# Token statistics of four more tiles on ScalarE, a weight expansion on GpSimd, the last product in two halves, and a new instruction order

## The chip, the cores and the metric

The kernel runs on one core of one Trainium2 chip. The metric is the device time of one execution in microseconds. One execution was also recorded by the hardware profiler; its rows are what the text argues from. The engines are called by what they do in the profile: PE is TensorE's matmuls and PEld its weight loads, DVE is VectorE, ACT is ScalarE, POOL is GpSimd, SP is SyncE, whose queue issues nearly all DMAs.

## The reference

Two layers over a sequence of S = 2048 tokens of width D = 640, in bf16. The first is a linear attention of H = 32 heads of width 20, with softmax feature maps; the second a bilinear gated feed-forward of width F = 1536. Both have a layer norm ahead and a residual around them.

```python
def _layernorm(x, axis=-1, eps=1e-5):
    m = jnp.mean(x, axis=axis, keepdims=True)
    v = jnp.var(x, axis=axis, keepdims=True)
    return (x - m) / jnp.sqrt(v + eps)

def _A_ref(x, wqkv, w_phi, wo):
    q, k, v = ...                      # x @ wqkv, split into 32 heads of 20
    pq = jnp.einsum("bhsd,hdf->bhsf", q, w_phi)
    pk = jnp.einsum("bhsd,hdf->bhsf", k, w_phi)
    phi_q = jnp.concatenate([_softmax(pq, axis=-1), _softmax(-pq, axis=-1)], axis=-1)
    phi_k = jnp.concatenate([_softmax(pk, axis=-1), _softmax(-pk, axis=-1)], axis=-1)
    kv = jnp.einsum("bhsf,bhsd->bhfd", phi_k, v)
    z  = jnp.einsum("bhsf->bhf", phi_k)
    num = jnp.einsum("bhqf,bhfd->bhqd", phi_q, kv)
    den = jnp.einsum("bhqf,bhf->bhq", phi_q, z)[..., None] + 1e-6
    return (num / den, heads side by side) @ wo

def _B_ref(x, w_gate, w_up, w_down):
    g = jnp.einsum("bsd,df->bsf", x, w_gate)
    u = jnp.einsum("bsd,df->bsf", x, w_up)
    return jnp.einsum("bsf,fd->bsd", g * u, w_down)

h  = x + _A_ref(_layernorm(x, axis=-1), A_wqkv, A_w_phi, A_wo)
h2 = h + _B_ref(_layernorm(h, axis=-1), B_w_gate, B_w_up, B_w_down)
```

## The kernel before, in words

The tokens are cut into 16 tiles of 128. Everything stays in SBUF from the loads to the last store. The kernel is written as a list of operations (`g.op`), each with its engine, what it reads and writes, the buffers it uses, and a planner's estimate of its length (`t`), of the time until others may use its result (`lat`), and, for DMAs, of the size. Nothing of that order reaches the chip as it is written: the table `ORDER` holds for each engine a string of unit names, and the n-th mention of a unit takes the n-th operation of that unit on that engine. So each engine's queue is written out by hand (or by a program), the engines run their queues strictly in order, and semaphores between them are placed where one needs another. The estimates decide only which of a pool's buffers an operation gets. Transposes and loads have eight semaphores each in turn (rings `tr` and `w`), stores of the result four (`out`). After its last DMA, SP waits for the last user of each of the twenty.

The units that the text speaks of:

- `wk`, `x0` to `x4`: the key weights are multiplied with the feature map's weights before any token is seen. `wk` are transposed chunks of the key weights with their column means, `x0` to `x4` the products. They need the expanded feature weights `Phi`, five pieces `a` (line 636), each a small product of two SBUF tensors; pieces 0 to 2 are made on VectorE, 3 and 4 on GpSimd. `y0` to `y4` do the same for the query weights, after five transposed loads `t0` to `t4` and mean additions `wq0` to `wq4`.
- `s0`, `s2`, `s4`, `s8`, `s12` (function `stats`): mean and square sum of the tokens, for 2, 2, 4, 4 and 4 tiles. There are two ways. For most, TensorE multiplies the transposed tile with itself and a column of ones, in five matmuls of 129 columns, and VectorE takes the diagonal of the product (line 702, one reduction a tile). For batches named in `ST_ACT`, TensorE only makes the column of sums, in five matmuls of one column, and ScalarE squares the untransposed tile with a running sum (line 650). The rest is small work on GpSimd.
- `k`, `v`, `q` with a tile number: products for keys, values and queries; VectorE takes a maximum for the exponentials and scales it (lines 925, 928), ScalarE takes two exponentials a tile for keys and queries (line 933) and copies the values. `K` and `Q`: sums of the features (lines 947, 987) and the scaling of the features, on GpSimd (line 950 for keys). `A`: the product of keys and values, in parts of two tiles, which ends this first part; `Aout` copies it.
- `n`, `h`: attention output of a tile, and its product with Wo, residual and second layer norm. `wo0` to `wo4`: row sums of Wo on ScalarE (line 650 too).
- `f`: the feed-forward's gate and up products. `d`, `D`: the down product; `D3.1` is the last, for tiles 14 and 15. A `D` unit makes seven half-size products into PSUM that are combined by additions on VectorE (lines 1332, 1342), with intermediate copies on ScalarE and additions on GpSimd.
- `lT4` to `lT15`: transposed loads of token tiles. `lx0` to `lx3`: plain loads of four token tiles each into `x_all` (640 KB). `lwq`, `lwo`, `lg`, `lu`, `ld`: weights.

PSUM is four buffers of two banks (`p_ps`), reused as soon as the engine that reads a product is done. The part of the last unit that the change rewrites is, before:

```python
mm(v2, 1, raw(3), wsum_(3), True)
fin(v2, 1, o2_, 0, c_)
store(o2_, t2)
mm(v2, 0, summed(3), wraw(3), False)
fin(v2, 0, o1_, 1, b_)
store(o1_, t1, 2 if b == NB - 1 else 1)
```

Of the kernel before, what the change touches and what calls it, by code (L numbers as in the profile page):

```python
# [1499 lines left out]
```

## Time and profile before

| what | value |
|---|---|
| runs, median (lowest to highest) | 267.58 us (267.44 to 268.17) |
| profiled execution | 267.55 us |
| its span, first to last instruction | 265.8 us |
| granted TensorE clock | 0.999 |
| TensorE busy | 260.4 us, 98% |
| VectorE, GpSimd, ScalarE busy | 222.7, 190.1, 177.2 us |
| DMA | 28.65 MB, mean 108 GB/s |

How to read it: the busy time of TensorE includes waits that matmuls hide in their pipeline, so the share alone does not say that it is at its limit. A row of the timeline gives start, length, engine, line, operation, result and sources with their sizes, and the number of instructions merged; a bracket at its end gives the idle time of that engine just before it and what ended it. A row of a window gives its length, then busy time and instruction count for PE, PEld, DVE, ACT and POOL, the clock, the share of the DMA engines and GB/s.

### The profile page before, as it was taken

The page shows a single profiled execution, that of the slowest core. Times are in us where ns is not written, and L with a number is a line of the kernel's source. Part 1 is how long each engine was busy: PE and PEld are TensorE (multiplying, and loading weights), DVE is VectorE, ACT ScalarE, POOL GpSimd, SP SyncE. Part 2 cuts the span into 40 slices and gives each one's busy share as a digit, 9 for nine tenths or more (in the row PEclk, how much of TensorE's full clock was granted, in tenths as well). Part 3 has the DMA queues.
Part 4 walks back from the last instruction along what each step waited for, and adds up shares of the span by engine and source line. Part 5 has one row for each costly group of instructions (what it writes and reads, how often), then busy time and mean ns, then how long its engine had stood idle before and what let it go on. Part 6 is the DMA issues. An engine that isn't in the chain of part 4 may idle for free.

```text
span 265.8 us, 6243 instructions
## 1 busy us (share of the span) xinstructions
PE 260.4 (98%) x2418; PEld 200.0 (75%) x2433; DVE 222.7 (84%) x417; ACT 177.2 (67%) x387; POOL 190.1 (72%) x243
## 2 busy tenths in 40 slices
PE   8999999999999999999999999999999999999995
PEld 8877777776877787777767887777777777777773
DVE  1999999999999876998999778988778788675683
ACT  2567999999857998769553695764857555645220
POOL 5446989999932889999974789359866575648652
PEclk9999999999999999999999999999999999999999
DMA  7997999903155789666856515300410401001012
GB/s 188 302 138 175 165 233 401 382 32 75 39 82 100 89 247 210 130 106 133 131 115 128 47 25 79 99 4 0 56 45 19 83 0 52 1 2 51 14 65 71
DMA packets 67390, 28.65 MB, mean 108 GB/s; under 512 B 57632, under 2 KB 66080, under 8 KB 67360
## 3 DMA queue, kind: packets, MB, share of 16 engines
q1 hardware_dynamic: 66432, 27.90, 48.7%
q10 hardware_dynamic: 928, 0.35, 0.5%
q8 instruction: 19, 0.31, 0.5%
q14 instruction: 11, 0.09, 0.1%
HBM read 11.82 MB, written 2.62 MB: 54 GB/s over the span
## 4 chain that ended last, share of the span: by engine, by line
PE 85%; DVE 5%; DMA 3%; ACT 3%; issue 1%; POOL 1%; SPq 0%; ACTq 0%
PE ps L657 60%; PE ps L1210 24%; DMA phiqT<-eq 3%; ACT eq L933 1%; DVE ob L1075 1%; PE ps L746 1%; DVE x_all L1093 1%; DVE ps L925 1%; DVE Sq L987 1%; ACT phiqT L1335 0%; POOL eq L999 0%; DVE rden L1073 0%; DVE phiqT L806 0%; ACT junk L650 0%; ACT eq L1220 0%
## 5 line engine op out<-in xcount | busy, mean ns | idle before, releaser
L657 PE MATMUL ps<-Wp,xT 128*128 128x320 bf16 (+1 forms) x606 | 89.1, 299 | 0.0
L657 PEld LDWEIGHTS ps<-Wp,xT 128*128 128x128 bf16 x606 | 58.0, 98 | 22.5 <-ACT phik L933 0.3
L1240 POOL TENSOR_TENSOR phik<-phik,gate 128x512 bf16<-128x512 bf16 x34 | 40.1, 1184 | 25.9 <-DVE phik L1237 25.5
L1220 ACT ACTIVATE eq<-ps 128x256 f32<-128x256 f32 x110 | 37.4, 386 | 23.0 <-PE ps L1210 18.6
L1210 PE MATMUL ps<-phik,Wgu 128*128 128x256 bf16 (+1 forms) x214 | 46.6, 299 | 0.2
L950 POOL TENSOR_TENSOR phik<-phik,Rk 128x1280 bf16<-128x1280 bf16 x16 | 37.4, 2357 | 5.8 <-DVE Rk L949 4.8
L657 PE MATMUL ps<-phik,Wgu 128*128 128x256 bf16 (+1 forms) x259 | 33.2, 280 | 0.1
L657 PEld LDWEIGHTS ps<-phik,Wgu 128*128 128x128 bf16 x260 | 25.0, 98 | 5.5
L1337 POOL TENSOR_TENSOR phiqT<-phiqT,x_all 128x320 f32<-128x320 f32 x26 | 21.7, 844 | 9.7 <-ACT phiqT L1335 9.6
L925 DVE TENSOR_REDUCE ps<-ps 128x1 f32<-128x640 f32 (+1 forms) x32 | 26.1, 818 | 2.8 <-PE ps L657 2.8
L1210 PEld LDWEIGHTS ps<-phik,Wgu 128*128 128x128 bf16 x228 | 21.9, 98 | 5.7 <-ACT eq L1220 0.2
L657 PE MATMUL ps<-vaug,phik 128*128 128x63 bf16 (+1 forms) x308 | 25.9, 238 | 0.0
L987 DVE TENSOR_REDUCE Sq<-eq 128x66 f32<-128x1320 bf16 x16 | 24.2, 1513 | 1.4 <-ACT eq L933 1.4
L1237 DVE TENSOR_TENSOR phik<-ps,eq 128x512 bf16<-128x512 f32 x28 | 19.1, 687 | 6.3 <-PE ps L1210 6.2
L1335 ACT ACTIVATE phiqT<-ps 128x320 f32<-128x320 f32 x26 | 11.4, 437 | 19.3 <-PE ps L657 19.2
L947 DVE TENSOR_REDUCE Ssum<-phik 128x64 f32<-128x1280 bf16 x16 | 23.3, 1460 | 0.0
L1235 DVE TENSOR_TENSOR gate<-ps,eq 128x512 bf16<-128x512 f32 x27 | 18.5, 685 | 5.2 <-PE ps L1210 2.9
L657 PEld LDWEIGHTS ps<-vaug,phik 128*128 128x128 bf16 x308 | 18.1, 97 | 5.3
L999 POOL TENSOR_TENSOR eq<-eq,rq 128x660 bf16<-128x660 bf16 x16 | 20.9, 1305 | 0.8
L933 ACT ACTIVATE eq<-ps,nb,rs 128x300 bf16<-128x300 f32 (+2 forms) x26 | 17.2, 689 | 6.1 <-DVE nb L928 4.5
L1342 DVE TENSOR_TENSOR outb<-ps,phiqT 128x320 bf16<-128x320 f32 x28 | 13.4, 487 | 6.9 <-PE ps L657 5.5
L1139 ACT ACTIVATE gate<-ps 128x256 bf16<-128x256 f32 (+1 forms) x26 | 10.4, 406 | 10.3 <-PE ps L657 9.6
(168 smaller groups left out, 526.2 us busy)
## 6 DMA issues: line engine op xcount, KB each, us to landing
x_all<-in_A_x_dram SPq DMA_DIRECT2D x4, 640.0 KB, 10.7
out_dram<-outb SPq DMA_DIRECT2D x14, 160.0 KB, 1.9
Wgu<-in_B_w_gate_dram SPq DMA_DIRECT2D x1, 1920.0 KB, 10.6
Wgu<-in_B_w_up_dram SPq DMA_DIRECT2D x1, 1920.0 KB, 16.3
vaug<-in_B_w_down_dram SPq DMA_DIRECT2D x1, 1920.0 KB, 8.5
Wp<-in_A_wqkv_dram SPq DMA_DIRECT2D x1, 800.0 KB, 5.0
phiqT<-in_A_wqkv_dram SPq DMA_DIRECT2D x1, 800.0 KB, 6.4
Wo<-in_A_wo_dram SPq DMA_DIRECT2D x1, 800.0 KB, 6.0
```

The costliest lines, as they stand in the source:

```text
L657: ins = e.matmul(o_, lhsT=l_, rhs=r_, start=s_, stop=p_, skip_group_check=True)
L925: g.op("DVE", lambda e: e.tensor_reduce(out=mx(), in_=src(), axis=AX.XY if len(src().shape) == 3 else AX.X, op=ALU.max, apply_absolute_val ...
L933: g.op("ACT", lambda e, s=s, sc=sc, to=to, of=of: e.activation(out=to(s), in_=of(), func=ACT.Exp, bias=nb[:, i:i + 1], scale=sc[:, t:t + 1 ...
L947: g.op("DVE", lambda e: e.tensor_reduce(out=Ssum[:, vs.i, :], in_=x, axis=AX.X, op=ALU.add), rd=R_phik[t], wr=vs.R, use=[vs], t=1.39, lat=1.5)
L950: g.op("POOL", lambda e: e.tensor_tensor(out=x, in0=x, in1=Rk[:, vr.i, :].unsqueeze(2).to_broadcast([P, 2 * H, DH]), op=ALU.mult), rd=vr.R ...
L987: g.op("DVE", lambda e: e.tensor_reduce(out=Sq[:, vs.i, :].rearrange("p (w g) -> p w g", w=NQ), in_=feat(0, NQ).rearrange("p w (g f) -> p ...
L999: return e.tensor_tensor(out=x, in0=x, in1=rq[:, vr.i, :].rearrange("p (w h) -> p w h", h=HW).unsqueeze(3).to_broadcast([P, NQ, HW, DH]), ...
L1210: ins = e.matmul(o_, lhsT=l_[0](c), rhs=m_, start=fr, stop=False, skip_group_check=True)
L1220: g.op("ACT", lambda e: e.activation(out=half(s[i], 256 * h, 256 * (h + 1)), in_=PS[v.i][:, bk, 256:512], func=ACT.Copy), rd=[v.R[bk]], wr ...
L1237: g.op("DVE", lambda e: e.tensor_tensor(out=hhT[:, hb_, ft, :], in0=PS[v.i][:, 1, :], in1=half(s[1]), op=ALU.add), rd=[v.R[1]] + s[1].R, w ...
L1240: g.op(eng, lambda e: e.tensor_tensor(out=hhT[:, hb_, ft, :], in0=hhT[:, hb_, ft, :], in1=gate[:, vg.i, :], op=ALU.mult), rd=R_out + vg.R, ...
L1337: g.op("POOL", lambda e: e.tensor_tensor(out=slot(x), in0=slot(x), in1=x_all[:, t, c], op=ALU.add), rd=x.R + [R_h[t]], wr=x.R, use=[x], t= ...
```

## The change

`ST_ACT` names batch 8 besides 12, so tiles 8 to 11 take the second way. The third piece of `Phi` moves from VectorE to GpSimd. In the last `D` unit the product that is made last is another one, and it is cut into two halves of 160 columns, each added and stored by itself; the stores of that unit go out in pieces, some of them on ScalarE's queue. All five engines' orders are new. The planner's estimates for loads and transposes are changed, which only matters for how buffers are dealt out.

```diff
-ST_ACT = (12,)
+ST_ACT = (8, 12)
...
-        g.op("DVE" if a < 3 else "POOL", phi_op, t=0.42, rd=[R_Wrows, R_G[a]], wr=[R_Phi[a]])
+        g.op("DVE" if a < 2 else "POOL", phi_op, t=0.42, rd=[R_Wrows, R_G[a]], wr=[R_Phi[a]])
...
-        def store(o_, t, parts=1):
+        def store(o_, t, parts=1, by=("SP", "SP")):
...
-                g.op("SP", lambda e, k=k: e.dma_start(out[0, P * t:P * (t + 1), n * k:n * (k + 1)], outb[:, o_.i, n * k:n * (k + 1)]),
+                g.op(by[k], lambda e, k=k: e.dma_start(out[0, P * t:P * (t + 1), n * k:n * (k + 1)], outb[:, o_.i, n * k:n * (k + 1)]),
...
+        if (b, i) == (NB - 1, 1):
+            g.op("SP", lambda e: e.dma_start(out[0, P * t2:P * (t2 + 1), HALF:D], outb[:, o2_.i, HALF:D]), rd=[o2_.R[1]], use=[o2_],
+                 dma=("w", 8), t=0.45, lat=0.1, size=0.2)
+        if (b, i) == (NB - 1, 1):
+            mm(v2, 0, summed(3), wraw(3), False)
+            fin(v2, 0, o1_, 1, b_)
+            store(o1_, t1, 2, ("SP", "ACT"))
+            l_, r_, q = raw(3), wsum_(3), HALF // 2
+            o_ = o2_
+            for k, (vk, bk) in enumerate(((v2, 1), (v1, 1))):
+                g.op("PE", lambda e, k=k, vk=vk, bk=bk: mms(e, [(PS[vk.i][:, bk, 0:q], l_[0](ft), r_[0](ft)[:, q * k:q * (k + 1)], ft == 0, False)
+                                                                for ft in range(KH)]), rd=l_[1] + r_[1], wr=[vk.R[bk]], use=[vk], t=0.415, lat=0.565)
+                R_q = Reg()
+                g.op("DVE", ...)       # adds PS[vk][:, bk, 0:q] and its part of c_ into outb
+                g.op(("ACT", "SP")[k], ...)       # stores these 160 columns
+            return
```

The orders, cut to the stretches that the prediction speaks of (TensorE's opening and the part about the statistics of tiles 8 to 11, ScalarE's middle, SP's loads, VectorE around `q7`):

```diff
 PE
-"warm wk wk wk wk wk wk wk wk wk s0 wk x1 s0 x1 x3 wv wv x2 x0 x0 s2 x4 s2 k0 ... s4 s4 s4 s4 v5 k7 v7 k4 k6 v4 k5 y3 v0 y1 s8 s8 s8 s8 y4 k10 y2 y0 v1 s12 ..."
+"warm wk wk wk wk wk wk wk wk wk x0 wk x1 x0 x1 s0 x3 s0 wv wv x2 x4 s2 s2 k0 ... s4 s4 s4 s4 k7 v4 v5 v7 k4 y1 k6 k5 y3 v0 s8 s8 s8 s8 k10 y4 y2 v1 s12 ..."
-"... f0.6.0 q10 f0.2.0 f0.3.0 q9 f0.9.0 f0.3.0 f0.9.0 n4 ..."
+"... q10 n5 f0.3.0 f0.3.0 f0.6.0 f0.6.0 n4 q9 f0.9.0 ..."
 ACT
-"... k1 v2 v3 k3 k2 wq1 k2 v5 wq3 k7 v7 k7 k4 k4 v4 k6 k6 k5 v0 k5 s12 ..."
+"... k1 v3 v2 k1 k2 s8 k2 s8 wq1 wq3 v5 v4 v7 k7 k7 k4 k4 s8 k6 s8 k5 v0 k6 k5 y4 y2 s12 ..."
-"... wo0 v14 k12 k12 v10 k13 wo1 k13 v13 k14 k14 wo2 v8 k15 k15 v15 q2 wo4 ..."
+"... wo2 v12 wo3 v10 k14 k14 k15 k15 q2 q2 v15 wo2 v8 q3 q3 wo0 wo1 wo4 ..."
 DVE
-"... n1 n1 q7 Q5 q7 Q5 q4 ..."
+"... n1 n1 q7 n1 q7 Q5 q4 ..."
 SP
-"in in in in in in in lwq t4 lT7 lT4 t2 lT5 lT6 t3 t1 t0 lx3 lT10 lT15 lT9 lT11 lT8 lT13 lT14 lT12 lx0 lwo lg lu lx2 lx1 Q0 ..."
+"in in in in in in in lT4 lwq lT6 lT5 lT7 lx2 t2 t3 t1 lT11 t0 t4 lx3 lT9 lT8 lT10 lT13 lT15 lT12 lT14 lx0 lwo lu lg Q1 Q0 Q1 Q0 lx1 ..."
```

More of the change, by code (lines that the diff above doesn't have):

```diff
@@ L587, in load_xT @@
     def load_xT(t, at=0.0):
-        transpose(lambda: xT[:, t, :, 0:P], lambda: A_x[0, P * t:P * (t + 1), :], [], [R_xT[t]], t=1.5, size=0.75, lat=1.25 if at else 2.75, at=at)
+        transpose(lambda: xT[:, t, :, 0:P], lambda: A_x[0, P * t:P * (t + 1), :], [], [R_xT[t]], t=1.5 if at else 1.4, size=0.75 if at else 0.62, lat=1.25 if at else 2.1, at=at)
     def load_x(b):
-        load(x_all[:, 4 * b:4 * b + 4, :], A_x[0, 4 * P * b:4 * P * (b + 1), :].rearrange("(t p) n -> p t n", p=P), [R_x[b]], 1.2)
+        load(x_all[:, 4 * b:4 * b + 4, :], A_x[0, 4 * P * b:4 * P * (b + 1), :].rearrange("(t p) n -> p t n", p=P), [R_x[b]], 0.9)
     def load_wv(c0, c1, at):
@@ L686, in f @@
                 return mms(e, lst)
-            g.op("PE", f, rd=[R_xT[t], R_one, R_xone], wr=[v.R[j // 2]], use=[v], t=0.125 if act else 0.282, lat=0.275 if act else 0.43)
+            g.op("PE", f, rd=[R_xT[t], R_one, R_xone], wr=[v.R[j // 2]], use=[v], t=0.19 if act else 0.282, lat=0.34 if act else 0.43)
             if act:
@@ L818, in wq_means @@
         v = Buf(p_ps, 2)
[L819 removed]
+        g.op("PE", lambda e: mms(e, mean_mms(PS[v.i][:, 0, :], range(NC), 0)), rd=R_Wnat + [R_one], wr=v.R, use=[v], t=0.73, lat=0.88)
         g.op("ACT", lambda e: e.activation(out=nmeanq[:, :], in_=PS[v.i][:, 0, 0:NC], func=ACT.Copy, scale=-1.0 / SC),
@@ L1362, in down_pair @@
         fin(v1, 0, o2_, 1, d_, [c_])
+        if (b, i) == (NB - 1, 1):
[11 more added lines that the diff above has]
+                R_q = Reg()
+                g.op("DVE", lambda e, k=k, vk=vk, bk=bk: e.tensor_tensor(
+                    out=outb[:, o_.i, q * k:q * (k + 1)], in0=PS[vk.i][:, bk, 0:q], in1=slot(c_)[:, q * k:q * (k + 1)], op=ALU.add),
+                    rd=[vk.R[bk]] + c_.R, wr=[R_q], use=[vk, o_, c_], t=0.28, lat=0.4)
+                g.op(("ACT", "SP")[k], lambda e, k=k: e.dma_start(out[0, P * t2:P * (t2 + 1), q * k:q * (k + 1)], outb[:, o_.i, q * k:q * (k + 1)]),
+                     rd=[R_q], use=[o_], dma=("w", 8), t=0.45, lat=0.1, size=0.1)
+            return
         mm(v2, 1, raw(3), wsum_(3), True)
@@ L1385, in _build @@
     U("lwo")
-    load(Wo[:, :, 0:D], A_wo.rearrange("(c p) n -> p c n", p=P), R_Wo, 1.5)
+    load(Wo[:, :, 0:D], A_wo.rearrange("(c p) n -> p c n", p=P), R_Wo, 0.95)
     for b in range(NB):
```

9 lines of the change are left out of this document (4 added, 5 removed), and 134 rows, old and new, of the table ORDER.

## The prediction

> **What bounds the kernel now.** I read the page first: busy time per engine, then the chain that ended last.
>
> ```profile
> PE 260.4 (98%) x2418; PEld 200.0 (75%) x2433; DVE 222.7 (84%) x417; ACT 177.2 (67%) x387; POOL 190.1 (72%) x243
> PE 85%; DVE 5%; DMA 3%; ACT 3%; issue 1%; POOL 1%; SPq 0%; ACTq 0%
> ```
>
> Then the chain in order of time, for the stretch in which the statistics, keys, values and first queries are made:
>
> ```profile
> 9.14 28.33 PE ps L657 x289
> 37.47 0.04 issue
> 37.51 2.08 PE ps L657 x26
> 39.59 0.02 issue
> 39.61 34.50 PE ps L657 x396
> 74.11 0.02 issue
> ```
>
> From 9.14 to 74.1 us the chain is TensorE itself. A busy PE can hide waits, since the ends of matmuls are modelled, so I compare issue rates, by rows of the timeline (start, length, instructions):
>
> ```profile
> 34.13 1.30 PE L657 MATMUL ps<-xT 128*128 128x129 bf16 x20
> 35.26 0.48 PE L657 MATMUL ps<-Phi,phiqT 128*128 128x140 bf16 x6
> 39.61 2.93 PE L657 MATMUL ps<-Wp,xT 128*128 128x320 bf16 x20
> 261.90 0.98 PE L657 MATMUL ps<-vaug,xT 128*128 128x320 bf16 x6
> ```
>
> Twenty 320-column matmuls in this stretch take 2.93 us, six in the kernel's last product 0.98, so one more costs (2.93 - 0.98) / 14 = 139 ns, 0.43 ns a column; twenty of 129 columns hold TensorE from 34.13 to 35.26, 1.13 us, 0.44 ns a column. The same pace for both: TensorE streams, it does not wait. So a shorter TensorE program gains time one for one, as long as the other engines follow. The windows say how far they can:
>
> ```profile
> 20.00:30.00 10.00, 10.00 (x88) 7.52 (x86) 9.60 (x25) 8.65 (x12) 7.25 (x9) 1.00 0.88 180
> 30.00:40.00 10.00, 9.94 (x110) 7.77 (x109) 9.97 (x24) 9.52 (x16) 8.95 (x10) 1.00 0.87 206
> 40.00:50.00 10.00, 10.00 (x83) 7.09 (x81) 10.00 (x19) 9.10 (x15) 9.61 (x11) 1.00 1.03 399
> 60.00:70.00 10.00, 10.00 (x141) 7.65 (x140) 10.00 (x17) 9.79 (x17) 9.92 (x6) 1.00 0.37 74
> ```
>
> The columns after the length are PE, PEld, DVE, ACT, POOL, clock, DMA share, GB/s. VectorE is full from 30 us on, GpSimd from 40, ScalarE nearly. Four engines run within a few per cent of each other: a cut on one is worth at most the slack of the next.
>
> **Part 1: squares of tiles 8 to 11 on ScalarE.** TensorE's five 129-column matmuls a tile become five of one column, and VectorE's reductions become ScalarE passes.
>
> ```profile
> 39.20 0.39 PE L657 MATMUL ps<-ones,xT 128*128 128x1 bf16 x10
> L657 PE MATMUL ps<-ones,xT 128*128 128x1 bf16 x20 | 0.8, 163 | 0.0
> L702 DVE CUSTOM_DVE_ANT_0 t<-ps,ident x12: 278/284/287, 9.0 to 37.2; 128x128 f32<-128x128 f32 x12
> L650 ACT ACTIVATE junk<-x_all x6: 728/749/809, 36.2 to 97.5; 128x640 bf16<-128x640 bf16 x6
> ```
>
> The twenty wide ones hold TensorE for 1.13 us (above). The narrow ones go out every (0.39 - 0.163) / 9 = 25 ns: twenty are 0.50. Relief **0.63 us**. VectorE loses four reductions, 0.28 each in their own rows. ScalarE gains four passes of 0.75: 3.0 us. In 20 to 50 us it has 1.35 + 0.48 + 0.90 = 2.73 us idle, so they fit only if nearly every gap can be used. I cost them at nothing: what hides them is that TensorE waits for no square, only for PSUM buffers that ScalarE has read, of which four are in turn; and that the new order leaves two row sums of Wo ahead of the last key tile instead of three. If that cover is gone, rival 2. Between ends of 0 and 3.0 I take 0, the value of today's four squares, which stand among the same gaps with TensorE at its pace.
>
> A second relief is in who held a buffer (the reductions of s8, first and last of four, and who waited):
>
> ```profile
> 36.53 0.28 DVE L702 CUSTOM_DVE_ANT_0 t<-ps,ident 128x128 f32<-128x128 f32 x1
> 37.16 0.28 DVE L702 CUSTOM_DVE_ANT_0 t<-ps,ident 128x128 f32<-128x128 f32 x1
> 37.51 0.31 PEld L657 LDWEIGHTS ps<-Phi,phiqT 128*128 128x128 bf16 x6 [0.22 <-DVE sxx L702]
> 37.54 0.22 POOL L708 TENSOR_SCALAR vpe<-sxx 128x4 f32<-128x4 f32 x1 [0.53 <-DVE sxx L702]
> 34.50 2.36 POOL L950 TENSOR_TENSOR phik<-phik,Rk 128x1280 bf16<-128x1280 bf16 x1 [0.30 <-DVE Rk L949]
> ```
>
> The four go out in 0.21 us each, 0.84 in all. Product y0 waited 0.2 us because VectorE's reductions still read the statistics' bank; after the change that bank is free once the sums are copied. I take **0.20 us**; bounds 0 (another bank is late, as ScalarE's now may be) and 0.22.
>
> [...]
>
> **What must follow.** Keys are scaled on GpSimd one tile after another, and the last one must end before the product with the values reads it:
>
> ```profile
> 63.13 9.30 POOL L950 TENSOR_TENSOR phik<-phik,Rk 128x1280 bf16<-128x1280 bf16 x4
> 72.33 1.77 PE L657 MATMUL ps<-vaug,phik 128*128 128x63 bf16 x55
> ```
>
> The fourth scaling ends at 72.43. Of the 55 matmuls, 34 come from the first that reads tile 15 to the last (10 + 12 + 12 by the code); the 21 ahead of it take 21 x 1.77 / 55 = 0.68 us at most, so it starts at about 72.95. GpSimd's slack is 0.5 us: TensorE may come that much earlier, and by as much again as GpSimd's own gaps close (0.53 waiting for the square sums, 0.30 for the reciprocal, above). 0.63 + 0.20 needs both. I take it as paid.
>
> **Part 2: third expansion on GpSimd.**
>
> ```profile
> 5.98 0.86 POOL L636 TENSOR_TENSOR Phi<-Wrows,G 128x140 bf16<-128x140 bf16 x2 [1.93 <-DMA Wrows<-in_A_w_phi_dram]
> 7.44 0.32 DVE L636 TENSOR_TENSOR Phi<-Wrows,G 128x160 bf16<-128x160 bf16 x1
> 7.59 0.74 POOL L777 CAST outb<-nmean 128x640 bf16<-128x640 f32 x1 [0.75 <-DVE nmean L775]
> 7.95 1.07 DVE L806 TENSOR_SCALAR phiqT<-ps,nmean 128x384 bf16<-128x384 bf16 x3 [0.19 <-PE ps L746]
> ```
>
> GpSimd does three instead of two, 5.98 + 3 x 0.43 = 7.27, within its 0.75 us idle. VectorE's 0.32 lay in a wait, since L806 waits for TensorE at 7.95 anyway: saved there, nothing. But x0 now stands ahead of the last transposition and needs all five expansions: it may start at 7.3 where TensorE is ready at 7.2, which makes L806 later by 0.1 to 0.2; against that, two x products (0.31 each) are done by then instead of one statistics tile (0.28). Taken as zero, bounds -0.35 and +0.2.
>
> **Part 3: the last product in halves.**
>
> ```profile
> 262.62 1.31 SPq L1349 DMA_DIRECT2D out_dram<-outb  x3
> 262.92 0.49 DVE L1342 TENSOR_TENSOR outb<-ps,phiqT 128x320 bf16<-128x320 f32 x1 [0.32 <-PE ps L657]
> out_dram<-outb SPq DMA_DIRECT2D x14, 160.0 KB, 1.9
> out_dram<-outb SPq DMA_DIRECT2D x4, 80.0 KB, 1.7
> L1148 DVE TENSOR_TENSOR phik<-ps,gate 128x256 bf16<-128x256 f32 x12 | 4.9, 413 | 1.9 <-ACT gate L1139 1.4 <-PE ps L657 0.5
> ```
>
> TensorE issues the same columns in twelve matmuls for six: +0.02. The addition after the last matmul has 160 columns: 0.49 at 320 and 0.41 at 256 make 1.2 ns a column, so 0.30; saved 0.19. Its store is issued on a queue that is free instead of behind two others (three issues fill 1.31 us), and one goes out by ScalarE, idle there; the landing I leave at 1.7, with -0.1 and +0.2 as bounds from the step between 160 and 80 KB. Net **-0.17**. [...]
>
> **Part 4: order and queues.** Two waits behind the first part lie where the diff changes the order:
>
> ```profile
> 81.56 0.39 PEld L657 LDWEIGHTS ps<-Phi,phiqT 128*128 128x128 bf16 x11 [0.43 <-ACT eq L933]
> 105.24 0.39 PEld L657 LDWEIGHTS ps<-Phi,phiqT 128*128 128x128 bf16 x11 [0.49 <-ACT eq L933]
> x_all<-in_A_x_dram SPq DMA_DIRECT2D x1, 640.0 KB, 4.7
> x_all<-in_A_x_dram SPq DMA_DIRECT2D x4, 640.0 KB, 10.7
> ```
>
> n2 waits for a buffer that q7's exponentials still read; these wait for q7's scaled maximum, which VectorE now makes ahead of Q5's sums and not behind them. n4 waits in the same way for q10, and moves ahead of q9, so with one buffer fewer taken. They could give up to 0.43 and 0.49 (idle of the weight loads); each could come back elsewhere, because every buffer is reused at once. I cost the reorder at nothing, bounds -0.9 and +0.9. The load of tokens 8 to 11 moves from nearly last on SP to behind lT7, issued near 13.5; it lands at 18.2 by the 4.7 us of its neighbour and at 24.2 by the median. The first square stands on ScalarE behind an exponential of k2, near 23 us, so I cost it at nothing; if it waits, k2's other exponential, wq1, wq3 and v5 wait behind it, and TensorE for their buffers. What the load is moved past, five transposed loads of Wq and the token tiles from 8 on, each wait up to 3.6 us more (640 KB at 180 GB/s). The wq additions on VectorE and then y1 need all five, and y1 stands two products (some 2.8 us) earlier than the first y product does now: cost nothing while the Wq tiles land before VectorE has done s4, k7 and K1, else rival 4.
>
> **Sum** against the profiled execution, 267.55 us (span 265.8; the median of the runs is 267.58, the same): 267.55 - 0.63 - 0.20 - 0.17 = **266.55**.
>
> **Rivals.**
> 1. GpSimd or VectorE sets the pace: the tile-15 scaling stays where it is, and TensorE gains nothing up to 73 us but waits there. For it: VectorE 10.00, GpSimd 9.92 of 10 us; against: both lose work or gaps. Left are the tail and at most the 0.5 of slack: 267.55 - 0.17 - 0 to 0.5, 266.9 to 267.4.
> 2. Slower: ScalarE is overrun. All four squares stand ahead of k5's exponentials, so before about 40 us, where the gaps from 20 us on total 1.35 + 0.48: 3.0 - 1.83 = 1.2 us late, and up to 3.0 if no gap is usable. TensorE, waiting for PSUM buffers, then loses as much. Against it: the row sum moved away, and 0.90 idle behind 40 us in which to catch up. It decides once the delay passes the gain of 1.0 and the 0.8 that can be told; at 3.0 the time is 267.55 + 3.0 - 1.0 = 269.55, at 1.2 it is 267.75.
> 3. The reorder also pays: half to all of n2's and n4's waits go, 266.55 - 0.46 to 0.92: 265.65 to 266.1.
> 4. The edit does not do what it says, because the early token load holds the Wq tiles up: a wait at y1 of 0.5 to 1 us, inside the 3.6 of the load: 267.05 to 267.55.
>
> **How the numbers follow.** Forecast 0.45 (own range 266.1 to 267.0), rival 1 0.23, rival 2 0.14, rival 3 0.10, rival 4 0.08. No change means within 0.3%, about what a measurement of this kernel can tell: 266.75 to 268.35. Faster: rival 3, and 0.37 of the forecast's 0.45, 0.47. Slower: the upper half of rival 2 and a little more, 0.11. Same: 0.42. The range 265.6 to 268.2 leaves out the far ends of rivals 2 and 3.
>
> **What would show it.** Twenty one-column matmuls for s8 in some 0.5 us and no VectorE reduction beside them; four ScalarE passes of 0.75 between 20 and 36 us; the last matmul of the value product at about 73.1 instead of 73.9; a last VectorE addition of 0.30 us. The prediction is wrong if TensorE's chain is broken between 20 and 48 us by ScalarE (rival 2), at tile 15 by GpSimd (rival 1), or by a landing of x_all or Wq (rival 4).

## The result, and the profile after

| | before | after |
|---|---|---|
| runs, median (lowest to highest) | 267.86 us (267.44 to 269.24) | 270.25 us (269.27 to 271.56) |
| ratio, 95% interval | | 1.0092 (1.0070 to 1.0115) |
| profiled execution, span | 267.55, 265.8 us | 270.22, 268.5 us |

Slower by 0.9%, where 0.4% faster was forecast. The changed kernel's page, busy times and the chain by engine:

```profile
PE 261.3 (97%) x2439; PEld 199.0 (74%) x2439; DVE 220.1 (82%) x409; ACT 180.9 (67%) x395; POOL 189.9 (71%) x244
PE 85%; DVE 6%; DMA 3%; ACT 2%; POOL 2%; issue 1%; SPq 0%; ACTq 0%
```

These lines hide the loss. VectorE is busy 2.6 us less, ScalarE 3.7 more, in the direction of the edit; TensorE looks no busier than before, because the modelled ends of matmuls swallow its pauses. So I took the starts of successive matmuls and counted what each step exceeds the usual one for its width (0.14 us at 320 columns, 0.11 at 256; steps of 0.33 us behind 256 columns, 15 of them before, as many as matmul records are missing there, are not counted). Added up, TensorE paused 4.1 us before and 7.6 us after: 3.5 more, against 0.6 less work and 0.2 less tail, which is the 2.7 us between the spans. By place, in us from the start of the span:

| mark | before | after | later by |
|---|---|---|---|
| first product of keys (k0) starts | 12.71 | 12.93 | 0.2 |
| statistics of batch 8 start | 34.07 | 34.91 | 0.8 |
| last weights of the value product (A14) end | 73.98 | 74.77 | 0.8 |
| h2 starts | 88.72 | 91.11 | 2.4 |
| last matmul ends | 262.88 | 265.78 | 2.9 |
| span | 265.8 | 268.5 | 2.7 |

The largest step is at h2. The changed kernel's waits of TensorE (total, times, longest):

```profile
PE ps L657 <- DMA phik<-ob: 1.2, 1, 1.2
...
PE ps L657 <- DVE sm L698: 0.8, 1, 0.8
PE ps L657 <- DVE nmean L775: 0.3, 1, 0.3
```

Its timeline there, with SyncE's DMA issues:

```profile
81.31 0.58 SPq L549 DMA_DIRECT2D vaug<-in_B_w_down_dram  x1
...
84.94 2.22 SPq L553 DMA_TRANSPOSE phik<-ob  x1
...
91.11 1.21 PEld L657 LDWEIGHTS ps<-Wo,phik 128*128 128x128 bf16 x10 [1.45 <-DMA phik<-ob]
```

The same two operations in the kernel before:

```profile
84.56 2.93 SPq L553 DMA_TRANSPOSE phik<-ob  x2
...
88.72 1.31 PEld L657 LDWEIGHTS ps<-Wo,phik 128*128 128x128 bf16 x10
```

h2 multiplies n2's output, which a transposing DMA brings into place. Before, that DMA was issued at 84.56 and landed at 87.20. After, it was issued at 84.94, 0.4 later, and landed at 91.07. In front of it on SyncE now stands `ld`, the load of the down weights. In the old order `ld` stood behind Q7 Q7 Q4; the diff moves it to directly behind Q3. DMAs issued from 81 to 92 us in the changed kernel (count, KB, median us to landing):

```profile
vaug<-in_B_w_down_dram SPq DMA_DIRECT2D x1, 1920.0 KB, 8.6
...
phik<-ob SPq DMA_TRANSPOSE x2, 4.4
```

The 4.4 is the median of two: the first, n2's, took 6.1 us, the second 2.7.

The same window of the kernel before:

```profile
phik<-ob SPq DMA_TRANSPOSE x2, 2.6
```

The second wait, 0.8 us in the view of waits and 0.94 by the starts, lies at k10, the product behind the statistics of batch 8. In the table the 0.6 us of saved work hides most of it:

```profile
34.77 1.48 DVE L947 TENSOR_REDUCE Ssum<-phik 128x64 f32<-128x1280 bf16 x1
34.91 0.58 PEld L657 LDWEIGHTS ps<-ones,xT 128*128 128x128 bf16 x20 [0.37 <-issue]
...
36.16 0.15 DVE L698 COPY sm<-ps 128x4 f32<-128x4 f32 x1
...
36.37 1.20 PEld L657 LDWEIGHTS ps<-Wp,xT 128*128 128x128 bf16 x10 [0.89 <-DVE sm L698]
```

The twenty narrow matmuls are there, in 0.58 us. Then k10 waits for their PSUM buffer until VectorE has copied the sums out (36.16 to 36.31), and that copy stands behind K7's sum of 1.48 us.

The theories that the runs were to tell apart: the load `ld` keeps transposes behind it from landing (theory 1); at k10 VectorE's order holds the buffer (2a), or ScalarE, late by its four squares (it is busy for 26.98 of the 27.00 us from 19 to 46), holds the others (2b); the opening loses by GpSimd's third expansion or by x0's place ahead of s0 (theory 3). The rival to all: the new order is late as a whole, and a wait taken away at one place comes back at the next.

### The profile page after: what moved, and what is told of

It is laid out like the page before. It is cut to its first block, busy times and chain, and to the rows that moved or that the text cites. A ratio compares the mean times of both kernels' runs of the same rounds, so it can differ in the third digit from the quotient of the medians.

```text
span 268.5 us, 6289 instructions
## 1 busy us (share of the span) xinstructions
PE 261.3 (97%) x2439; PEld 199.0 (74%) x2439; DVE 220.1 (82%) x409; ACT 180.9 (67%) x395; POOL 189.9 (71%) x244
## 4 chain that ended last, share of the span: by engine, by line
PE 85%; DVE 6%; DMA 3%; ACT 2%; POOL 2%; issue 1%; SPq 0%; ACTq 0%
PE ps L657 60%; PE ps L1210 25%; DMA phiqT<-in_A_wqkv_dram 2%; DMA vaug<-ob 1%; POOL eq L999 1%; ACT eq L933 1%; DVE phiqT L1164 1%; ACT hb L1119 1%; DVE Sq L987 1%; DVE ps L925 1%; DVE phik L1148 1%; DVE x_all L1107 1%; DVE ob L1075 1%; POOL phik L1145 0%; PE ps L746 0%
## 5 line engine op out<-in xcount | busy, mean ns | idle before, releaser
L1220 ACT ACTIVATE eq<-ps 128x256 f32<-128x256 f32 x110 | 38.3, 385 | 28.5 <-PE ps L1210 27.8
L1240 POOL TENSOR_TENSOR phik<-phik,gate 128x512 bf16<-128x512 bf16 x34 | 39.4, 1164 | 22.1 <-DVE phik L1237 22.0
L1210 PE MATMUL ps<-phik,Wgu 128*128 128x256 bf16 (+1 forms) x228 | 50.6, 304 | 0.0
L657 PE MATMUL ps<-phik,Wgu 128*128 128x256 bf16 (+1 forms) x260 | 33.9, 281 | 0.1
L925 DVE TENSOR_REDUCE ps<-ps 128x1 f32<-128x640 f32 (+1 forms) x32 | 26.3, 824 | 2.6 <-PE ps L657 2.2
```

The lines of the kernel that those rows point to most:

```text
L657: ins = e.matmul(o_, lhsT=l_, rhs=r_, start=s_, stop=p_, skip_group_check=True)
L925: g.op("DVE", lambda e: e.tensor_reduce(out=mx(), in_=src(), axis=AX.XY if len(src().shape) == 3 else AX.X, op=ALU.max, apply_absolute_val ...
L1210: ins = e.matmul(o_, lhsT=l_[0](c), rhs=m_, start=fr, stop=False, skip_group_check=True)
L1220: g.op("ACT", lambda e: e.activation(out=half(s[i], 256 * h, 256 * (h + 1)), in_=PS[v.i][:, bk, 256:512], func=ACT.Copy), rd=[v.R[bk]], wr ...
L1240: g.op(eng, lambda e: e.tensor_tensor(out=hhT[:, hb_, ft, :], in0=hhT[:, hb_, ft, :], in1=gate[:, vg.i, :], op=ALU.mult), rd=R_out + vg.R, ...
```

## The experiments

Every ratio is to the kernel before, run in turn on the same chip. The last column is TensorE's pauses in the profiled execution, counted as above (4.1 before, 7.6 after). That execution is not always near the kernel's median: for "before, ld behind Q3" it took 271.7 us (median 269.6), for "before, squares on ScalarE" 271.1 (269.1), for "ld in four, short K7 sum" 267.5 (268.2); the others lie within 0.7 us.

| kernel | ratio (95%) | pauses |
|---|---|---|
| after, ld behind Q7 Q7 Q4 | 1.0083 (1.0066 to 1.0099) | 7.1 |
| after, ld behind Q4 Q4 | 1.0112 (1.0089 to 1.0135) | 8.1 |
| after, ld in four | 1.0028 (1.0015 to 1.0041) | 5.8 |
| before, ld behind Q3 | 1.0098 (1.0060 to 1.0136) | 8.3 |
| before, ld behind Q4 Q4 | 1.0045 (1.0033 to 1.0057) | 5.4 |
| after, copy s8 ahead of K7 | 1.0107 (1.0092 to 1.0122) | 8.0 |
| after, both moves | 1.0111 (1.0091 to 1.0131) | 8.3 |
| before, squares on ScalarE | 1.0072 (1.0048 to 1.0096) | 8.3 |
| after, without those squares | 1.0126 (1.0106 to 1.0146) | 8.0 |
| ld in four, short squares | 1.0029 (1.0018 to 1.0041) | 5.6 |
| ld in four, short squares, copy first | 1.0047 (1.0033 to 1.0060) | 5.9 |
| ld in four, short K7 sum | 1.0030 (1.0018 to 1.0042) | 4.9 |
| before, third Phi on GpSimd | 1.0001 (0.9992 to 1.0010) | 3.8 |
| ld in four, old opening | 1.0136 (1.0123 to 1.0150) | 9.2 |
| before, tail in halves | 1.0001 (0.9989 to 1.0013) | 4.6 |
| before, ld behind Q4 Q4, tail | 1.0031 (1.0019 to 1.0042) | 5.0 |
| before, ld in four, Phi, tail | 1.0042 (1.0029 to 1.0054) | 5.2 |
| before, Phi, tail, q7's bias first | 1.0001 (0.9989 to 1.0013) | 4.3 |

### The load of the down weights

The changed kernel with `ld` back in its old place:

```diff
-"... Q3 Q3 ld Q5 n2 Q5 n3 Q7 Q7 Q4 Q4 n7 ..."
+"... Q3 Q3 Q5 n2 Q5 n3 Q7 Q7 Q4 ld Q4 n7 ..."
```

> The changed kernel with one token moved: SyncE issues the down-weight load (ld, 1.92 MB) behind Q7 Q7 Q4 again, as the kernel before does, in place of directly behind Q3. Theory 1 (the early load holds up the transpose that n2's output goes through, so h2 waits): the wait of 1.3 us at h2 falls under 0.2 us and the time falls by 1.0 to 1.3 us against the changed kernel, to about 269.0 (0.4% above the kernel before). Rival (h2's wait is the slack of an order that is late as a whole, and whatever stands there waits for something else): h2 or its neighbours still wait about a microsecond and the time stays within 0.3 us of the changed kernel.

h2's wait went, as expected, and the time hardly moved: a wait of 1.5 us stood at n4 instead, which needs the second transpose of Q4. It was issued at 95.09, behind `ld`, and landed at 103.36, just after `ld` (102.66). The converse, in the kernel before:

```diff
-"... Q3 Q3 Q5 Q5 n2 n3 Q7 Q7 Q4 ld Q4 ..."
+"... Q3 Q3 ld Q5 Q5 n2 n3 Q7 Q7 Q4 Q4 ..."
```

> The kernel before with one token moved: SyncE issues ld directly behind Q3, as the changed kernel does. Theory 1: n2's transpose lands some 3 to 4 us later than its 87.2 us, h2 waits about 1 us, and the time rises by 0.8 to 1.3 us over the kernel before. The rival (lateness of the whole order): no wait at h2, time within 0.3 us of the kernel before.

One token, and the old kernel is as slow as the new one. The wait was twice the forecast, and more came behind it. TensorE's weight loads in its timeline:

```profile
91.60 3.97 PEld L657 LDWEIGHTS ps<-Wo,phik 128*128 128x128 bf16 x18 [2.53 <-DMA phik<-ob]
```

Its windows (after the length: PE, PEld, DVE, ACT, POOL with counts, then the granted clock):

```profile
85.00:89.00 4.00, 4.00 (x37) 3.30 (x36) 3.93 (x8) 2.73 (x8) 2.10 (x3) 1.00 1.13 302
89.00:91.50 2.50, 0.35 (x4) 0.07 (x1) 1.19 (x3) 1.61 (x4) 2.06 (x5) 1.00 1.23 195
91.50:95.20 3.70, 3.60 (x15) 2.12 (x16) 0.89 (x2) 1.25 (x4) 1.03 (x2) 0.55 1.03 88
```

After the pause TensorE was granted 0.55 of its clock for 3.7 us, and fourteen matmuls took 0.27 us each and not 0.14: another 1.7 us of loss. That belongs to this execution, whose mean clock was 0.993, and, by its mean clock, to one more of the six (0.994, 272.3 us). The other four had a mean clock of 0.999 to 1.0, which leaves no room for such a stretch, and still took 268.9 to 270.0 us, 1.4 us or more above the kernel before (267.4). Next, the changed kernel with `ld` one place further back:

```diff
+"... Q3 Q3 Q5 n2 Q5 n3 Q7 Q7 Q4 Q4 ld n7 ..."
```

> The changed kernel with ld behind both transposes of Q4, one place further than in the run that moved it behind the first of Q7 Q7 Q4. Theory 1, sharper (while the 8.5 us load is under way no transpose lands, and the price is that of whichever product first needs a transpose queued behind it): h2 (1.3 us) and n4 (1.5 us with ld ahead of the second Q4) both stop waiting; next behind ld stands n7, whose product h7 comes at about 106 to 108 us, when the load has landed (some 104). The time falls by 1.2 to 1.6 us against the changed kernel, to 0.35 to 0.5% above the kernel before. Rival (the order is late as a whole, a wait moves on wherever ld goes): a wait of about 1 us appears at h7, n6 or f0.x behind 104 us and the time stays within 0.4 us of the changed kernel.

The rival's place, by the theory's mechanism. A wait of 1.9 us stood at the product f0.2.0, as the timeline shows:

```profile
105.44 0.83 DVE L1075 TENSOR_TENSOR ob<-ps,rden 128x640 bf16<-128x640 f32 x1 [2.33 <-DMA vaug<-ob]
...
106.32 0.22 PEld L657 LDWEIGHTS ps<-phik,Wgu 128*128 128x128 bf16 x3 [1.98 <-DVE ob L1075]
```

n7's transpose, issued behind `ld`, landed at 105.35; until then it held one of the two `ob` buffers, so VectorE could not divide n4, so n4's PSUM buffer stayed taken, so f0.2.0 had none. I had followed only the product that reads the transposed tile, not the buffer that the transpose reads from. In the kernel before the same place (with T0, which reads these weights, a little later on GpSimd) also lost:

```diff
-SP "... Q7 Q7 Q4 ld Q4 Q6 ..."      POOL "... Q8 T0 h0 f0.2.0 f0.3.0 T0 h1 ..."
+SP "... Q7 Q7 Q4 Q4 ld Q6 ..."      POOL "... Q8 h0 f0.2.0 f0.3.0 T0 T0 h1 ..."
```

> The kernel before with ld behind the second transpose of Q4 in place of ahead of it, and on GpSimd the first T0 (which reads the loaded weights) two steps later, beside the second, so that it does not hold up the gate products. Theory 1: n4's wait of 0.38 us at 104.8 us goes, nothing else changes: 0.2 to 0.4 us faster than the kernel before (267.0 to 267.2 on this chip). Rival: h7 or n6 wait in its place, time equal or up to 0.5 us more.

Its pauses were 0.3 us at 95 and 110 us and 0.7 at 134, none of them at n4. Their rows name ScalarE, GpSimd and VectorE, none a DMA, and T0 was moved as well, so this loss is not shown to be the load's. No place tried for the whole load was better than that of the old order. In the traces of both kernels a transpose issued behind the 1.92 MB landed after them: in the kernel before the load landed at 101.96 and the next transpose, issued at 94.10, at 102.64; in the changed kernel the load landed at 89.90 and the next transpose, issued at 83.22, at 90.49. Whether that is what costs was tried by cutting the load:

```diff
+    for f0 in range(0, NF, 3):
+        ...  # Wd[:, f0:f0 + 3, :], rows P * f0 to P * (f0 + 3)
-"... Q3 Q3 ld Q5 n2 Q5 n3 Q7 Q7 Q4 Q4 n7 ..."
+"... Q3 Q3 ld Q5 n2 Q5 n3 ld Q7 Q7 ld Q4 Q4 ld n7 ..."
```

> The changed kernel with the down-weight load ld cut into four loads of three row blocks each, issued behind Q3, n3, the second Q7 and the second Q4. Theory 1 (transposes land only when the load ahead of them has; each quarter holds them for some 2 us and not 8.5): the waits seen at h2 (1.3 us, whole load behind Q3), n4 (1.5, ahead of the second Q4) and h7 (1.9, behind Q4) are all under 0.3 us, and the time falls by 1.2 to 1.6 us against the changed kernel, to 0.35 to 0.5% over the kernel before. Rival (what waits there waits for the lateness of VectorE, ScalarE or GpSimd, and a transpose that comes earlier only moves the wait on): some wait of about a microsecond stays between 84 and 112 us, time within 0.5 us of the changed kernel.

DMAs of that kernel from 80 to 98 us:

```profile
vaug<-in_B_w_down_dram SPq DMA_DIRECT2D x4, 480.0 KB, 4.7
...
phik<-ob SPq DMA_TRANSPOSE x2, 2.6
```

Its longest waits of TensorE:

```profile
PE ps L657 <- PEq L1506: 0.8, 1, 0.8
PE ps L657 <- DVE sm L698: 0.8, 1, 0.8
PE ps L657 <- issue: 0.3, 1, 0.3
```

The waits at h2, n4 and f0.2.0 are all gone, and 1.0092 became 1.0028: 0.64%, 1.7 us: some two thirds of the loss. For these waits the rival falls: none came back elsewhere. (The 0.8 us of PEq lies ahead of the first matmul and is in every kernel here.)

### The statistics of batch 8, and k10

The copy moved ahead of the sum on VectorE, alone and with `ld` moved back:

```diff
-"... k5 K7 s8 K4 K7 ..."
+"... k5 s8 K7 K4 K7 ..."
```

> The changed kernel with one token moved on VectorE: the copy of batch 8's statistics out of PSUM (s8) stands ahead of K7's sum of 1.48 us and no longer behind it. Theory 2a (the copy's place holds the buffer that k10 waits for): k10's wait of 0.94 us falls to about 0.3, time -0.4 to -0.6 us, unless K7, which gets 0.9 us later, is missed further on. Theory 2b (ScalarE is late by the four squares, 3 us of work, and holds the neighbouring buffers of k5, k6 and v0 until 36.7 to 38.2 us): the wait moves to the next product behind k10, and the time stays within 0.2 us of the changed kernel.

> Both tokens moved in the changed kernel. If the two waits are independent, the time falls by the sum of the two single moves (theory 1 with 2a: -1.5 to -1.8 us, to about 268.6; theory 1 with 2b: -1.0 to -1.3). If a wait that is gone at one place comes back at the other (VectorE's lateness from the K7 sum carries to the attention output), the pair gives less than the sum.

k10's wait fell from 0.94 to 0.39 us, as 2a says. But v1, three products later, now waits for ScalarE's exponentials. The weight loads of k10 and v1 with the copy first:

```profile
35.69 1.20 PEld L657 LDWEIGHTS ps<-Wp,xT 128*128 128x128 bf16 x10 [0.34 <-DVE sm L698]
...
38.15 1.20 PEld L657 LDWEIGHTS ps<-Wp,xT 128*128 128x128 bf16 x10 [0.47 <-ACT phik L933]
```

Another 0.4 us stands at 52 us, behind exponentials that waited 0.27 us for VectorE's bias, which they did not without the move. Nothing was gained, and the pair gained nothing either. Part 1 by itself, in the kernel before:

```diff
-ST_ACT = (12,)
+ST_ACT = (8, 12)
-ACT "... k3 k2 wq1 k2 v5 wq3 ... v4 k6 k6 k5 ..."      DVE "... K4 s8 s8 s8 s8 s8 K4 ..."
+ACT "... k3 k2 s8 wq1 k2 s8 v5 wq3 ... v4 s8 k6 s8 k6 k5 ..."      DVE "... K4 s8 K4 ..."
-SP "... lT7 lT4 t2 lT5 ... lg lu lx2 lx1 ..."
+SP "... lT7 lT4 lx2 t2 lT5 ... lg lu lx1 ..."
```

> The kernel before with part 1 alone: squares of tiles 8 to 11 on ScalarE (four activations, two behind k2 and two beside k6), VectorE without their four reductions, the token load lx2 early on SyncE, nothing else moved. Theory 2b (ScalarE, without an idle stretch there, hands the 3 us on to the exponentials and so to the PSUM buffers that k10 waits for): a wait of 0.5 to 1.5 us at k10 or its neighbours, and the time 0 to 0.9 us above the kernel before in spite of 0.63 us less TensorE work. The prediction's own account (the squares lie beside other work): 0.6 to 0.8 us faster. Theory 2a (the order of VectorE alone is to blame): also about 0.6 us faster, since VectorE keeps its order here.

The load of the tokens that the squares read, `lx2`, moves ahead here too; no wait of TensorE or ScalarE from 20 to 41 us is for a DMA. 2b was right about this kernel, and its size went beyond the range given. TensorE's weight loads in the timeline:

```profile
30.21 2.56 PEld L657 LDWEIGHTS ps<-Wp,xT 128*128 128x128 bf16 x20 [0.63 <-ACT vaug L956]
...
34.75 0.31 PEld L657 LDWEIGHTS ps<-Phi,phiqT 128*128 128x128 bf16 x6 [0.31 <-DVE Wp L864]
...
36.23 0.58 PEld L657 LDWEIGHTS ps<-ones,xT 128*128 128x128 bf16 x20 [1.16 <-issue]
...
37.62 0.40 PEld L657 LDWEIGHTS ps<-Wp,xT 128*128 128x128 bf16 x3 [0.58 <-DVE sm L698]
```

Two windows of it:

```profile
35.00:37.00 2.00, 0.99 (x30) 0.84 (x28) 1.94 (x3) 2.00 (x5) 1.69 (x1) 1.00 0.49 79
37.00:41.00 4.00, 3.60 (x23) 2.26 (x21) 1.58 (x4) 2.70 (x5) 3.63 (x10) 0.57 1.05 379
```

ScalarE, with two squares done by then, frees v7's buffer late (30.2); the product behind it is late, so VectorE's maximum is late, so its copies y3 and y1 are late, and the narrow statistics wait for them. k10 then waits for VectorE's copy of the sums. The saved 0.6 us on TensorE turns into waits, and in this execution the clock falls to 0.57 behind them. Four of the six ran at a mean clock of 1.0 and took 268.9 to 269.1 us, some 1.5 us above the kernel before (267.5). The reverse, the changed kernel without part 1:

```diff
-ST_ACT = (8, 12)
+ST_ACT = (12,)
-ACT "... k2 s8 k2 s8 wq1 ... k4 s8 k6 s8 k5 ..."      DVE "... K7 s8 K4 ..."
+ACT "... k2 k2 wq1 ... k4 k6 k5 ..."      DVE "... K7 s8 s8 s8 s8 s8 K4 ..."
```

> The changed kernel without part 1: the squares of tiles 8 to 11 are sums on VectorE and TensorE again (ScalarE without its four squares, VectorE with four reductions at the place of the copy s8, TensorE with the 129-column products, 0.63 us more of work); the new orders stay. Theory 2b (the squares make ScalarE late): k10's wait of 0.94 us goes or falls under 0.3 us, as does the 0.16 us at 51 us, and in spite of the 0.63 us of work the time falls by 0.2 to 0.6 us against the changed kernel. Theory 2a (VectorE's order holds the buffer): the wait grows to some 1.5 us (VectorE has 0.9 us more to do before it frees it), and the time rises by about 1 us.

The time rose by 0.9 us, as 2a had it, but not for its reason: k10's wait did not grow, it fell from 0.94 to 0.45 us, though not under 2b's 0.3. From the first keys to 65 us the pauses hardly change in all: less at k10, 0.4 more at 42 and 0.2 more at 52 us, behind the four reductions that VectorE has to do again. TensorE's 0.6 us of work are back, and behind h2, at 93 us, ScalarE is waited for by 0.8 us more. So taking part 1 out of the new order does not make it faster, but this run does not tell 2a from 2b. For that, one piece of work was shortened at a time, with nothing moved, on the kernel with the load in four. First ScalarE's squares:

```diff
-act_sum(x_all[:, t, :], ACT.Square, ...)
+act_sum(x_all[:, t, 0:64 if i0 == 8 else D], ACT.Square, ..., scale=3.1623 if i0 == 8 else 1.0)
```

> The changed kernel with the load in four, where the four squares of batch 8 on ScalarE run over 64 columns of each row and not 640 (left out: nine tenths of the sum of squares; scaled up instead), so that ScalarE has some 2 us less to do and every order stays as it is. Theory 2b (ScalarE's lateness holds the buffers): s8's wait of 0.23 us and k10's of 0.94 us both fall, together by 0.7 us or more, and the time by 0.5 to 1.0 us against the changed kernel with the load in four. Theory 2a (VectorE's copy s8 behind K7's sum holds k10's buffer): k10's wait stays above 0.7 us, time within 0.3 us.

In its timeline, K7's sum and k10's first weights:

```profile
34.64 1.48 DVE L947 TENSOR_REDUCE Ssum<-phik 128x64 f32<-128x1280 bf16 x1
...
36.24 1.20 PEld L657 LDWEIGHTS ps<-Wp,xT 128*128 128x128 bf16 x10 [0.89 <-DVE sm L698]
```

2 us less on ScalarE, and k10 waits as long as ever; the time did not move. 2b falls for this order. With the copy first as well:

> The same with the copy s8 ahead of K7's sum on VectorE as well. If both hold buffers (2a and 2b, each alone only lets the wait move to the other): the waits between 30 and 60 us fall by a microsecond or more together, and the time is 0.3 us or more below that of the short squares alone. Under 2b alone: no better than the short squares, or 0.2 to 0.5 us worse, since K7 comes 0.9 us later (0.5 us at 51 us when the copy was moved alone).

Worse, as when the copy was moved alone. v1's wait was 0.23 us here and not 0.45, since ScalarE has less to do, but 0.4 us stood at 41.7, for VectorE's next copy. Then VectorE's sum, shortened:

```diff
-e.tensor_reduce(out=Ssum[:, vs.i, :], in_=x, ...)
+e.tensor_reduce(out=Ssum[:, vs.i, :], in_=x[:, :, 0:5] if t == 7 else x, ...)
```

> The changed kernel with the load in four, where VectorE's sum of K7 runs over 5 of the 20 columns of each group (left out: three quarters of that one sum), so that it takes some 0.4 us and not 1.47; every order and all the rest stays. Theory 2a (k10 waits for the buffer that the copy s8 frees, and the copy stands behind this sum): k10's wait falls from 0.94 to some 0.3 us (the statistics products end at 35.35), VectorE is 1 us earlier from there on, so the waits at 51 and 60 us do not grow: 0.6 to 0.8 us faster than the changed kernel with the load in four, equal to the kernel before within 0.3 us. Rival (another engine holds the buffers, as theory 2b had it): the wait moves to the next product, gain under 0.2 us.

The same rows of this kernel, and v1's:

```profile
34.51 0.48 DVE L947 TENSOR_REDUCE Ssum<-phik 128x64 f32<-128x320 bf16 x1
...
35.35 0.16 DVE L698 COPY sm<-ps 128x4 f32<-128x4 f32 x1 [0.36 <-PE ps L657]
...
35.56 1.20 PEld L657 LDWEIGHTS ps<-Wp,xT 128*128 128x128 bf16 x10 [0.34 <-DVE sm L698]
...
38.03 0.39 PEld L657 LDWEIGHTS ps<-Wp,xT 128*128 128x128 bf16 x4 [0.47 <-ACT phik L933]
```

k10 starts 0.7 us earlier, and three products later v1 waits 0.47 us for ScalarE's exponentials. The time did not move either. So VectorE holds the buffer that k10 waits for, and right behind it ScalarE is late by about as much: two engines at their limit in one stretch, and relief of one only shows the other. Both short at once was not tried, so the size of the pair stays open.

### The opening, the tail, and a better version

Part 2 alone, then part 3 alone, in the kernel before:

```diff
-g.op("DVE" if a < 3 else "POOL", phi_op, ...)
+g.op("DVE" if a < 2 else "POOL", phi_op, ...)
```

> The kernel before with part 2 alone: the third weight expansion on GpSimd, behind its other two. The prediction's account: 0, between -0.35 and +0.2 us. Theory 3 (the third expansion makes TensorE's first expansion products wait on GpSimd): TensorE's x1 waits about as long as now, since VectorE's third ends at 7.75 us there and GpSimd's would end near 7.3: no loss, the opening 0 to 0.3 us earlier. If x1 or k0 come 0.2 us later than before, part 2 costs that by itself; if not, the 0.2 to 0.3 us that the changed kernel loses there comes from its order (x0 ahead of s0).

```diff
-mm(v2, 1, raw(3), wsum_(3), True)
+...  # the last unit as in the change; on TensorE and VectorE one D3.1 more, on ScalarE two
```

> The kernel before with part 3 alone (last product in two halves, last stores on two queues). The prediction's account: -0.17 us; the last VectorE addition 0.30 us in place of 0.49. Rival (the halves' extra issue and landing eat it): equal within 0.1 us. From the last TensorE product to the end of the span it was 2.9 us before.

Both are no change that can be told: 1.0001 each. For part 2 k0 starts at 12.69 instead of 12.71. For part 3 the timeline of the changed kernel's end shows that the step itself works:

```profile
264.78 0.99 PE L657 MATMUL ps<-xT,phik 128*128 128x160 bf16 x12
...
265.40 0.74 DVE L1376 TENSOR_TENSOR outb<-ps,phiqT 128x160 bf16<-128x160 f32 x2
...
266.17 0.33 SPq L1379 DMA_DIRECT2D out_dram<-outb  x1
```

From the last matmul's end (265.78) to the end of the span are 2.71 us; before, 262.88 to 265.8, 2.92. That is 0.2 us, and it stands in every profile here: 2.6 to 2.7 us with part 3, 2.9 without. It is under what the times of the runs can tell (in the profiled execution of part 3 alone the opening, waiting 0.5 us for a weight load, hid it). The tail was also run beside `ld` behind Q4 Q4:

> b_ld_q4 with part 3 as well (the last product in two halves and the stores on two queues). The prediction's account of the tail: 0.17 us less than b_ld_q4; the last VectorE addition takes about 0.30 us. Rival (the extra store's issue and landing take the gain back): equal to b_ld_q4 within 0.1 us.

1.0031 against 1.0045, in the forecast direction, the intervals overlapping. The old opening in the changed kernel, load in four:

```diff
 PE
-"... x0 wk x1 x0 x1 s0 x3 s0 wv wv x2 x4 s2 s2 k0 ... k3 k1 wm v3 v2 k2 s4 ..."
+"... s0 wk x1 s0 x1 x3 wv wv x2 x0 x0 s2 x4 s2 k0 ... k3 k1 wm k2 v2 v3 s4 ..."
 DVE
-"... wk x1 s0 s0 s0 x3 c2 c0 s2 s2 c3 k0 k0 s2 c1 k3 c4 k1 k3 K0 k1 K0 K3 ..."
+"... wk s0 s0 x1 x3 s0 c2 c1 c0 s2 s2 c4 s2 k0 k0 c3 k3 k3 k1 k1 K0 K0 K3 ..."
 ...
```

> The changed kernel with the load in four and with the opening order (up to the batch of tiles 4 to 7) of the kernel before on TensorE, VectorE, ScalarE and GpSimd. Theory 3 (the changed opening costs by itself): x0's wait of 0.2 to 0.5 us, s0's 0.4, and those at 15.5 and 17 us (0.13 and 0.21) go; 0.2 to 0.5 us faster than the changed kernel with the load in four, to about 0.1 to 0.2% over the kernel before. Rival (the opening is bound by its loads, the waits change their place only): within 0.15 us of the changed kernel with the load in four.

In the opening itself theory 3 holds: x0's and s0's waits went, 0.45 us stood at a later expansion product instead, and k0 started at 12.54, 0.26 us earlier than with the new opening (12.80). What that is worth at the end stays open, since the seam between the old opening and the new continuation cost 2.9 us at 25 and 30 us. Finally two attempts to beat both kernels:

```diff
-SP "... Q3 Q3 Q5 Q5 n2 n3 Q7 Q7 Q4 ld Q4 Q6 ..."
+SP "... Q3 Q3 ld Q5 Q5 n2 n3 ld Q7 Q7 ld Q4 Q4 ld Q6 ..."
```

> The kernel before with the down-weight load in four (behind Q3, n3, the second Q7 and the second Q4), and with parts 2 and 3 (third expansion on GpSimd, last product in two halves), without part 1 and without the new orders. Theory 1: the wait at n4, where a run shows it, goes (0 to 0.4 us), the tail gives 0.2 us, part 2 nothing: 0.2 to 0.6 us faster than the kernel before. Rival (the kernel before already hides its load; three more issues on SyncE cost 0.58 us each and delay the transposes behind them): equal to it or up to 0.5 us slower.

Slower by 1.1 us, more than even the rival gave. The same four places that suit the new order put 1.3 us of wait at n7, which the old order has earlier; its longest wait:

```profile
PE ps L657 <- DMA phiqT<-eq: 1.2, 1, 1.2
```

The last one moves q7's bias ahead of Q5's sum on VectorE, as the prediction read n2's wait:

```diff
-DVE "... q7 Q5 q7 Q5 q4 ..."
+DVE "... q7 q7 Q5 Q5 q4 ..."
```

> The kernel before with parts 2 and 3 and one token moved on VectorE: q7's bias (nb, 0.14 us) ahead of Q5's sum (1.52 us) and no longer behind it. ScalarE's exponentials of q7 start at 80.05 in place of 80.5 us, and n2's wait for the buffer that they free (0.26 to 0.37 us at 81 us) goes; the tail gives 0.2 us: 0.3 to 0.6 us faster than the kernel before. Rival (each gain is taken up by the next wait, as with the other single moves): equal within 0.3 us.

From its timeline:

```profile
78.28 0.16 DVE L928 TENSOR_TENSOR nb<-ps,rs 128x1 f32<-128x1 f32 x1
...
80.12 0.90 ACT L933 ACTIVATE eq<-ps,nb,rs 128x660 bf16<-128x660 f32 x1 [0.44 <-DMA phiqT<-eq]
```

The bias is made 1.1 us sooner than in the kernel before (79.37 there) and ScalarE starts no sooner: it waits for an `eq` buffer, which Q2's second transpose frees on landing (80.01). The row of the kernel before says the same:

```profile
79.82 0.90 ACT L933 ACTIVATE eq<-ps,nb,rs 128x660 bf16<-128x660 f32 x1 [0.35 <-DMA phiqT<-eq]
```

No version beat the kernel before.

## Why the prediction was wrong

- **Part 4, order and queues** ("I cost the reorder at nothing, bounds -0.9 and +0.9") is the step that failed. It counted what the token load is moved past on SyncE, and not that `ld` moves too, past Q5, n2, Q5, n3, Q7, Q7 and Q4. The term was put at nothing; the one place was worth 1.3 us at h2, and the load in four gives back 1.7 us of the 2.5. Shown by the runs on `ld`: early in the old order it makes that kernel as slow, in four in the new order its waits are gone. Of the 1.0 us that the sum takes off, 0.6 of matmuls and 0.2 of tail are there; it has no term for the 3.5 us of new pauses.
- In the same part n2's and n4's waits did go, as rival 3 hoped (0.26 and 0.38 us in the profile). But a wait of 0.28 us stands at n3 in place of n2's, and n2's was read wrongly: q7's exponentials waited for a transpose, as their row in the kernel before names it (above), and not for q7's scaled maximum. And n4's comes and goes without an edit: the two runs that leave the order there alone, parts 2 and 3 by themselves, do not show it.
- **Part 1, relief of 0.63 us**: the matmuls take about what was said (0.58 us for 0.50), and the relief is real work gone. The cover failed: "they fit only if nearly every gap can be used", and in the old order they do not fit (rival 2's mechanism, +0.72% by itself, 1.9 us; 1.5 in the executions at full clock). In the new order ScalarE is not what k10 waits for; VectorE's copy behind K7's sum is, and the 3.0 us of bound did not name that order. y0's 0.20 us went, as forecast, and came back fourfold at k10. The value product's last matmul was put at 73.1 and came at 74.8.
- **What must follow** (GpSimd's slack at tile 15) was never tried, since TensorE came later, not earlier. Rivals 1 and 4 did not occur: the last Wq tile landed at 26.3 us, and y1 did not wait.
- **Part 2, zero**: right alone. In the changed kernel x0, now first, waits some 0.5 us (0.1 was said), until 0.1 us behind the third expansion's end (7.29), and k0 is 0.2 us late, the upper bound. The row names VectorE's `nmean`, which ends at the same time; with the load in four x0 starts before `nmean` is done, again 0.1 us behind the expansion.
- **Part 3, -0.17**: right, 0.2 in the traces; the last addition takes 0.33 us (0.30 was said). The two 40 KB stores, with rows of 320 B, land in 1.7 us, the 80 KB ones beside them in 1.6 to 2.0.
- What remains, 0.28% with the load in four, lies in the pauses of the opening (0.4 us more than before), at k10 (0.8), and in waits of 0.1 to 0.6 us from 50 to 60 and 130 to 150 us; the last differ from kernel to kernel where the order is the same, and their causes were not settled.

## What to carry to other kernels

When an order changes, list every DMA that changed its place, with its bytes, and price it by the transposes that are queued behind it: behind the load of 8.6 us n2's transpose took 6.1 us to land and not 2.6, and what first needed such a transpose, or a buffer that one still read, paid (1.45 us at h2, 2.0 at f0.2.0). Cut such a load and spread it (1.0092 became 1.0028), but fit the places to the order at hand: the same four cost the old order 0.4%. Where VectorE and ScalarE were both without a gap (each busy for 2.00 of 2.00 us from 35 to 37), reordering VectorE or shortening its sum showed only ScalarE's limit: k10's wait fell from 0.89 to 0.34 us, v1 then waited 0.47, and no time was gained; and moving squares to ScalarE cost the old order 0.72%. Shorten one piece of work at a time to see which, before believing the engine that the wait names.
